# One Trainium2 core: attention's kv product moved beside the second half of a feed-forward block, queries transposed in pairs

## The chip, the cores and the metric

The kernel runs on one core of one Trainium2 chip. The metric is the device time of one execution in microseconds. Before the change it is 605.95 us, the median of three runs (605.42 to 606.97). A core has TensorE (PE; matmuls and, in a list of its own, their weight loads, PEld), VectorE (DVE), ScalarE (ACT), GpSimd (POOL) and SyncE (SP), which here issues every DMA.

## What is computed

```python
def _A_ref(x, wqkv, wo):                  # linear attention, H = 32 heads of Dh = 16
    qkv = (x @ wqkv).reshape(B, S, 3, H, Dh).transpose(2, 0, 3, 1, 4)
    q, k, v = qkv[0], qkv[1], qkv[2]
    phi = lambda t: jnp.where(t > 0, t + 1, jnp.exp(t)) + 1e-6
    pq, pk = phi(q), phi(k)
    kv = jnp.einsum("bhsd,bhse->bhde", pk, v)
    z = jnp.einsum("bhsd->bhd", pk)
    num = jnp.einsum("bhqd,bhde->bhqe", pq, kv)
    den = jnp.einsum("bhqd,bhd->bhq", pq, z)[..., None] + 1e-6
    return (num / den).transpose(0, 2, 1, 3).reshape(B, S, D) @ wo

xn = _layernorm(x)
s = _A_ref(xn, wqkv, wo)
g = _silu((_gelu(xn @ w_gate) * (xn @ w_up)) @ w_down)
out = x + s * g
```

The shapes are B = 1, S = 2048 tokens, D = 512, F = 1792, all in fp32.

## The kernel before, in words

**Products.** A large product is cut into 2 x 2 blocks and made with seven block products instead of eight (the table PRODUCTS; products 1 to 7 below are its entries), so sums and differences of blocks ("forms") are needed on both sides. Every fp32 form is split into a high and a low part of a type that TensorE multiplies in one pass, and a product is the sum of high x high, high x low and low x high: `sum3` (L508 is its matmul) issues three matmuls of 128x512 for each pair of operands. Splits are a cast on ScalarE (L486) and a subtraction on VectorE or GpSimd (L492).

**Stages.** (1) The start: 16 token tiles are normalised, transposed and turned into forms; k and q are projected, phi(q) goes to DRAM (`q_d`), and G = xnᵀ·phi(k) is summed in four PSUM banks and stored (`g_d`). v itself is never made: kv is the product of v's weights and G. (2) The feed-forward block in two halves of the tokens, p = 1 and then p = 0. Each has 14 "quads" (seven units of F, gate and up for each) of seven products, named FX, FY and FZ by their PSUM tiles, and the products with w_down in groups (DX, DY, DZ), added into `acc`. In half p = 1 the forms of the weights are made by GpSimd, ScalarE and VectorE from raw weights and stored to DRAM; half p = 0 loads them again (w, wd). At the boundary of the halves the forms of xn for the second half are loaded (Xh, Xl), and so far also GT and wv (`attn_loads`); `attn_first` sums z, makes kv (pkv, L1250; masked to each head's 16 x 16 block), multiplies it with wo to a matrix M (pm, L1264), and M's forms are made and stored (m_d). (3) `queries(i)`, eight times in half p = 0: two token tiles of phi(q) are loaded, multiplied with z on GpSimd (u), summed to den, inverted and normalised on VectorE, transposed on TensorE (ptq, L1165), copied by ScalarE and stored (pn_d). (4) The last stage: forms of pn times M's forms (ms) in four quads of two halves and two column blocks, SX, SY, SZ and SV by their tiles; `block` adds a product to a saved one, multiplies with silu of the feed-forward block (g, acc), adds x (xp) and stores.

**What sets the order.** Nothing is issued when it is written. `do` records each operation with its engine, a cost and what it reads and writes; class Plan then simulates all five engines, gives each operation a due time and lists it by these. The pe_keys rank TensorE's operations only as a first setting. STEPS is a list of random seeds: each one shifts the due times in a short stretch of the program by a random amount. So the order on every engine comes from the costs and STEPS together, and each engine, SP with its single DMA queue among them, executes its list strictly in turn. `in_turn` binds operations of given keys to a stated order.

**Places in SBUF and PSUM.** `D2(12)` to `D2(14)` are the three places RAW through which raw weights pass in half p = 1; queries use them for q, u and the transposed pT; before the change so do wv, wo, M and the temporaries of M's forms. `ring` hands out places in rotation, and an operation that reuses one waits for the last user. WAYS and ON_POOL say for each block of the last stage which engine multiplies ("C": GpSimd) and adds x, and "B" that the product is written over g.

The touched functions, with line numbers as in the profile:

## Time and profile before

| | before |
|---|---|
| median of three runs | 605.95 us |
| profiled execution: time | 606.77 us |
| profiled execution: span of the records | 605.10 us |
| TensorE busy | 593.9 us, 98% |
| weight loads | 489.1 us, 81% |
| VectorE busy | 479.0 us, 79% |
| GpSimd busy | 353.9 us, 58% |
| ScalarE busy | 336.2 us, 56% |
| granted TensorE clock, mean | 0.998 |
| moved by DMA | 143.14 MB, mean 237 GB/s |

The span runs from the first to the last record; 1.67 us of the profiled execution's time lie around it. In a row of the timeline stand the start, the busy time, the engine, line, operation, output<-inputs and the count; in brackets the engine's idle time ahead of it and what ended that. A matmul's record runs past its issue, so the next one's start shows the pitch better than the duration. In the rows of waits stand the total, the number and the longest. A DMA row gives the size of one transfer and the median time from issue to landing.

### The profile page before, as it was taken

Reading aid. Unit: us, or ns where it says so; the run is one execution under the profiler, and the core shown is the slowest. Engines: PE = TensorE matmul, PEld = TensorE weight load, DVE = VectorE, ACT = ScalarE, POOL = GpSimd, SP = SyncE. Lnnn points to the kernel's source line nnn. Section 1 sums busy time; section 2 is a strip of 40 time slices with the busy share of each in tenths; the row PEclk is TensorE's granted clock in tenths of the full one; section 3 lists DMA queues with packets and bytes.
Section 4 is the critical chain, followed back from the end, with each engine's and each line's share of the span. In section 5 each row is a group of like instructions: output and inputs, shape, how many; then the busy total and the mean of one; then the engine's idle time right before and its main releaser. Section 6 shows DMA issues by size and latency. Waiting matters only on the chain.

```text
span 605.1 us, 8228 instructions
## 1 busy us (share of the span) xinstructions
PE 593.9 (98%) x2696; PEld 489.1 (81%) x2696; DVE 479.0 (79%) x700; ACT 336.2 (56%) x610; POOL 353.9 (58%) x298
## 2 busy tenths in 40 slices
PE   8999999999999999999999999999999999999996
PEld 7888888888888888887888878788888888887875
DVE  6999988785688987889879654767865986587997
ACT  6767878866666744654554154645404550477740
POOL 3925754552588976876787042648704670559455
PEclk9999999999999999999999999999999999999999
DMA  7269621358648747863869879988639774998536
GB/s 257 83 210 305 207 71 71 121 165 324 225 157 310 264 157 265 326 223 125 285 242 354 310 249 414 407 278 271 197 134 323 244 238 130 323 309 308 199 131 251
DMA packets 58794, 143.14 MB, mean 237 GB/s; under 512 B 5504, under 2 KB 17024, under 8 KB 58752
## 3 DMA queue, kind: packets, MB, share of 16 engines
q1 hardware_dynamic: 58752, 142.63, 67.3%
q8 instruction: 21, 0.34, 0.2%
q14 instruction: 21, 0.17, 0.1%
HBM read 81.00 MB, written 61.60 MB: 236 GB/s over the span
## 4 chain that ended last, share of the span: by engine, by line
PE 85%; DMA 9%; DVE 3%; ACT 1%; issue 0%; SPq 0%; POOL 0%; DVEq 0%; ACTq 0%
PE FX L508 22%; PE DX L508 11%; PE FZ L508 11%; PE gps L508 7%; PE FY L508 6%; PE X L508 5%; PE DZ L508 5%; PE Z L508 3%; PE SX L508 3%; PE DY L508 2%; PE q L508 2%; DMA m_d<-m 2%; DMA GT<-g_d 1%; PE SZ L508 1%; PE k L508 1%; PE Y L508 1%
## 5 line engine op out<-in xcount | busy, mean ns | idle before, releaser
L508 PE MATMUL FX<-Xh,w 128*128 128x512 f32 x448 | 150.9, 390 | 0.0
L1073 POOL TENSOR_TENSOR h<-h,g 128x512 f32<-128x512 f32 x42 | 62.9, 1498 | 89.8 <-DVE h L492 81.0
L508 PEld LDWEIGHTS FX<-Xh,w 128*128 128x128 f32 x448 | 83.9, 188 | 17.6 <-DVE w L492 0.3
L492 POOL TENSOR_TENSOR h<-h,h 128x512 f32<-128x512 f32 x56 | 86.5, 1545 | 12.3 <-ACT g L1065 1.8
L508 PE MATMUL FX<-Xl,w 128*128 128x512 f32 x224 | 87.3, 390 | 0.0
L508 PE MATMUL FZ<-Xh,w 128*128 128x512 f32 x224 | 77.4, 391 | 0.0
L486 ACT COPY fu<-FX 128x512 f32<-128x512 f32 x56 | 32.9, 588 | 74.3 <-PE FX L508 60.3
L508 PE MATMUL gps<-pks,xns 128*128 128x512 f32 x192 | 51.0, 391 | 0.0
L508 PEld LDWEIGHTS FX<-Xl,w 128*128 128x128 f32 x224 | 42.1, 188 | 8.7
L508 PEld LDWEIGHTS FZ<-Xh,w 128*128 128x128 f32 x224 | 41.8, 188 | 8.5
L508 PE MATMUL FZ<-Xl,w 128*128 128x512 f32 x112 | 43.9, 392 | 0.0
L753 POOL TENSOR_TENSOR zacc<-zacc,kp 128x512 f32<-128x512 f32 x16 | 25.2, 1574 | 31.7 <-DVE kp L742 31.3
L1099 DVE TENSOR_TENSOR acc<-acc,DX 128x512 f32<-128x512 f32 x48 | 32.5, 683 | 13.2 <-PE DX L508 12.7
L508 PEld LDWEIGHTS gps<-pks,xns 128*128 128x128 f32 x192 | 35.8, 188 | 7.4
L508 PE MATMUL FY<-Xh,w 128*128 128x512 f32 x112 | 39.6, 394 | 0.0
L492 DVE TENSOR_TENSOR h<-fu,FZ 128x512 f32<-128x512 f32 x28 | 19.2, 685 | 18.5 <-PE FZ L508 9.4
L1065 ACT ACTIVATE g<-g 128x512 f32<-128x512 f32 x42 | 26.6, 633 | 12.4 <-DVE g L492 12.3
L1099 DVE TENSOR_TENSOR acc<-acc,DZ 128x512 f32<-128x512 f32 x32 | 21.8, 685 | 14.5 <-PE DZ L508 13.9
L508 PE MATMUL X<-kq,Xh 128*128 128x512 f32 x96 | 31.8, 397 | 0.0
L492 POOL TENSOR_TENSOR u<-q,zacc 128x512 f32<-128x512 f32 x16 | 22.0, 1395 | 13.6 <-DMA q<-q_d 13.4
L492 DVE TENSOR_TENSOR g<-fu,FZ 128x512 f32<-128x512 f32 x28 | 19.1, 683 | 13.0 <-PE FZ L508 7.1
L492 POOL TENSOR_TENSOR T<-xt 128x256 f32<-128x256 f32 x16 | 13.7, 856 | 19.6 <-DVE kq L492 11.5
(422 smaller groups left out, 1600.7 us busy)
## 6 DMA issues: line engine op xcount, KB each, us to landing
w_d<-w SPq DMA_DIRECT2D x36, 512.0 KB, 4.9
w<-w_d SPq DMA_DIRECT2D x36, 512.0 KB, 5.0
wd_d<-wd SPq DMA_DIRECT2D x21, 512.0 KB, 4.8
wd<-wd_d SPq DMA_DIRECT2D x21, 512.0 KB, 5.2
x<-in_first SPq DMA_DIRECT2D x16, 256.0 KB, 3.3
q_d<-qp SPq DMA_DIRECT2D x16, 256.0 KB, 2.3
q<-q_d SPq DMA_DIRECT2D x16, 256.0 KB, 4.3
pn_d<-pT SPq DMA_DIRECT2D x8, 512.0 KB, 5.5
```

The source lines that it names most:

```text
L486: do("ACT", act(n), lambda o, i: nc.scalar.copy(o, i), dst, src, name=name)
L492: do(eng, c, lambda o, p, q: getattr(e, f"tensor_{op}")(o, p, q), dst, a, b, name=name)
L508: nc.tensor.matmul(o, v[i], v[i + 1], start=start and part == 0 and i == 0, stop=stop and part == 1 and i == len(v) - 2, skip_group_check=on)
L753: do("POOL", pool(D), lambda o, i: nc.gpsimd.tensor_add(o, o, i), zacc, p0, name="zacc")
L1065: curved("gelu", do("ACT", curve(NC), lambda o, i: nc.scalar.activation(o, i, AF.Gelu_apprx_tanh), g, ps if e is None else g, name="gelu"))
L1073: do("POOL", pool(NC), lambda o, i: nc.gpsimd.tensor_mul(o, o, i), h, g, name="h")
L1099: do("DVE", dve(NC), lambda o, i: nc.vector.tensor_add(o, o, i), a, ps, name="acc")
```

## The change

(1) `attn_loads` and `attn_first` are cut up. `z_part` stays at the boundary. `kv_part`, recorded beside quad 5 of half p = 0, loads v's weights and G in four pairs through RAW (wvg0 to wvg3), and one TensorE operation for each pair adds its four products into one bank; `m_part` makes the mask, the masked kv and M, with two pairs of wo through RAW, and stores M's raw values to a new DRAM array (mr_d). `m_forms`, beside quads 6 and 8, loads them again, makes the forms and stores them. (2) In `queries` the transposes of both token tiles are one TensorE operation. The planner's cost for the transposes of xn at the start is also another. (3) In the last quad the bank Z is copied by ScalarE (sz5) ahead of its block (1,1), and the end is fixed as products 6, 5, 7, then 3, then the two halves of 4. (4) Three blocks of the last stage are done in other ways: (0,0,1) goes over g with its addition on GpSimd, (1,0,0) has its multiply on GpSimd, (1,1,1) returns to VectorE, and (2,1,1) adds on GpSimd. (5) STEPS is another list, so the order changes everywhere.

```diff
-    STEPS = (11, 15, 18, 27, 48, 58, 91, 94, 107, ...)
+    STEPS = (28, 30, 51, 59, 73, 79, 109, 133, 151, ...)
...
-        do("PE", 0.432, run, pt, xns[t], ident, key=("T", n, i), name="T")
+        do("PE", 0.52, run, pt, xns[t], ident, key=("T", n, i), name="T")
...
-            pt = bank(ring("ptq", [5, 6, 7]), f"ptq{t}", (P, KT, P))
...
-            do("PE", 0.432, run_t, pt, half(q, n), ident, key=("QT", i, n))
-            copy("ACT", pTs[:, :, n * P:(n + 1) * P], pt, D, "pqT")
+        pts = [bank(ring("ptq", [5, 6, 7]), f"ptq{t0 + n}", (P, KT, P)) for n in range(2)]
+
+        def run_t(o, a, b, c, idn):
+            for v, u in ((o, b), (c, a)):
+                for k in range(KT):
+                    nc.tensor.transpose(v[:, k, :], u[:, k * P:(k + 1) * P], idn)
+        do("PE", 0.95, lambda o, a, b, idn: run_t(o, b, a, pts[1](), idn), pts[0], half(q, 0), half(q, 1), ident, more=(pts[1],), key=("QT", i))
+        for n in range(2):
+            copy("ACT", pTs[:, :, n * P:(n + 1) * P], pts[n], D, "pqT")
...
+            if not p and n in BESIDE:
+                keys += BESIDE[n]()
...
+    def kv_part():
+
+        pkv = kv_state["pkv"] = bank(5, "pkv", (P, KT, P))
+        for c in range(KT):
+            t = raw_pair(f"wvg{c}")
+            dma(half(t, 0), ext(first[PLACE["v", c]]), 256)
+            dma(half(t, 1), g_d(c, (slice(None), c)), 256)
+
+            def run_kv(o, a, b, c=c):
+                for g in range(KT):
+                    nc.tensor.matmul(o[:, g, :], a[:, g * P:(g + 1) * P], b[:, g * P:(g + 1) * P],
+                                     start=(c == 0 and g == 0), stop=(c == KT - 1 and g == KT - 1), skip_group_check=True)
+            do("PE", 0.95, run_kv, pkv, half(t, 0), half(t, 1), key=("kv", c))
+        return [("kv", c) for c in range(KT)] + m_part()
+
+    def m_part():
+
         mask2 = U("fe", FE, "mask2", F32, (P, P))
         do("POOL", 1.5, make_mask, mask2)
...
+           kv4, kv_state["pkv"], mask2)
+        for a in range(2):
+            wo_t = raw_pair(f"wo{a}")
+            pms = []
+            for h in range(2):
+                g = 2 * a + h
+                dma(half(wo_t, h), ext(wo_k[:, g]), 256)
+                pms.append(bank(6 + h, f"pm{g}"))
+                do("PE", 0.95, lambda o, a, b, g=g: nc.tensor.matmul(o, a[:, g, :], b, start=True, stop=True),
+                   pms[-1], kv4, half(wo_t, h), key=("m", g))
+            raw = raw_pair(f"m{a}")
+            for h in range(2):
+                copy("ACT", half(raw, h), pms[h], D, "M")
+            dma(mr_d(a, a), raw, 512, "store")
+        return [("m", g) for g in range(KT)]
+
+    def m_forms(a):
+        raw = raw_pair(f"mr{a}")
+        dma(raw, mr_d(a, a), 512)
+        ws = weights("D", a + 1, f"m{a}")
+        make_weights(ws, raw, D_BLOCKS, f"m{a}")
+        keep_weights(("m", a), ws)
+        return []
+
+    mr_d = dram_view([2, P, 2, D], "mr_d", 2)
+    BESIDE = {5: kv_part, 6: lambda: m_forms(0), 8: lambda: m_forms(1)}
...
-    attn_loads()
-    raws = attn_first()
+    z_part()
...
-    for a in range(2):
-        ws = weights("D", a + 1, f"m{a}")
-        make_weights(ws, raws[a], D_BLOCKS, f"m{a}", 12)
-        keep_weights(("m", a), ws)
...
-    WAYS = {(1, 0, 0): "B", (1, 1, 1): "B", (2, 0, 1): "B", (2, 1, 0): "B", (2, 1, 1): "B", (3, 0, 0): "C", (3, 1, 1): "B"}
-    ON_POOL = ((1, 0, 0), (1, 1, 1), (2, 0, 1), (2, 1, 0), (3, 0, 0), (3, 1, 1))
+    WAYS = {(2, 1, 1): "B", (3, 0, 0): "C", (3, 1, 1): "B", (2, 0, 1): "B", (1, 0, 0): "C", (2, 1, 0): "B", (0, 0, 1): "B"}
+    ON_POOL = ((0, 0, 1), (1, 0, 0), (2, 0, 1), (2, 1, 0), (2, 1, 1), (3, 0, 0), (3, 1, 1))
...
+        z5 = esaved(Z, f"sz5_{n}") if last else Z
         prod_s(X, 7, False)
         u3 = esaved(X, f"su3_{n}")
-        block(1, 1, u3, Z, V)
+        block(1, 1, u3, z5, V)
...
-            pe_keys += [("S", p, c, i) for i in (6, 7, 5, 3)] + [("S", p, c, 4, h) for h in range(2)]
+            end = [("S", p, c, 3), ("S", p, c, 4, 0), ("S", p, c, 4, 1)]
+            pe_keys += [("S", p, c, i) for i in (6, 5, 7)] + end
+            in_turn(end)
```

The first place is SP's queue at the boundary. Before, G's pieces (GT, from g_d) and v's weights (wv) stand among the loads of X, and the first queries' load q8 stands far behind, among the stores of M's forms (m_d) and loads of weights:

```order
L461 DMA GT0_3327<-g_d_81 128x512
L461 DMA Xl0_265<-xl_d_83 128x1024
L461 DMA Xh0_251<-xh_d_82 128x1024
L461 DMA GT2_3340<-g_d_81 128x512
L461 DMA GT1_3347<-g_d_81 128x512
...
L461 DMA wv23_3368<-in_first 128x512 x2
L461 DMA GT3_3381<-g_d_81 128x512
...
L461 DMA wd61_3705<-wd61_d_160 128x512
L461 DMA m12_d_169<-m12_3673 128x1024
L461 DMA q8_3714<-q_d_80 128x512 x2
```

Now SP's queue has there:

```order
L461 DMA wd53_d_159<-wd53_3092 128x1024
L461 DMA draw6_3145<-in_w_down 128x1024
L461 DMA Xl0_268<-xl_d_83 128x1024
L461 DMA Xh0_255<-xh_d_82 128x1024
L461 DMA q8_3245<-q_d_80 128x512 x2
L461 DMA Xh0_255<-xh_d_82 128x1024
L461 DMA Xl0_268<-xl_d_83 128x1024
```

GT, wv, wo and M's stores are gone from the boundary, and q8's load stands behind the first two loads of X.

The second place is SP's queue near quads 7 and 6 of the second half (w7, w6), now: wvg2 takes the place that pT12, the transposed queries 12 and 13, leaves with the store to pn1_d.

```order
L461 DMA pn1_d_85<-pT12_4038 512x1x256
L461 DMA w70_4062<-w70_d_128 128x1024
L461 DMA w61_4074<-w61_d_125 128x512
L461 DMA wvg2_4087<-in_first 128x512
L461 DMA wvg2_4087<-g_d_81 128x512
L461 DMA w63_4104<-w63_d_127 128x1024
L461 DMA wvg3_4114<-in_first 128x512
L461 DMA wvg3_4114<-g_d_81 128x512
L461 DMA wo0_4123<-in_wo 128x512 x2
L461 DMA w72_4142<-w72_d_130 128x1024
L461 DMA w73_4162<-w73_d_131 128x1024
L461 DMA wo1_4168<-in_wo 128x512 x2
```

TensorE's list there, behind kv's last products, now:

```order
L1265 MATMUL pm0_4196<-wo0_4123,kv_4171 128x512
L508 MATMUL DX050_4186<-hf5l_3876,wd50_3376 128x512
L508 MATMUL DX050_4186<-hf5h_3850,wd50_3376 128x512
L508 MATMUL DX050_4186<-hf4h_4117,wd40_3812 128x512
L508 MATMUL DX050_4186<-hf4l_4126,wd40_3812 128x512
L508 MATMUL DX050_4186<-hf4h_4117,wd40_3812 128x512
L1265 MATMUL pm2_4211<-wo1_4168,kv_4171 128x512
L1265 MATMUL pm3_4215<-wo1_4168,kv_4171 128x512
```

M's four products stand between the feed-forward products, five of which separate pm0 from pm2 in the same bank.

The third place is the end of TensorE's list. Before, product 4's last half and then product 3 (SZ3):

```order
L508 MATMUL SX3_5663<-sf1l_5564,ms11_5257 128x256
L508 MATMUL SX3_5663<-sf1h_5540,ms11_5257 128x256
L508 MATMUL SZ3_5747<-sf0h_5488,ms03_5184 128x512
L508 MATMUL SZ3_5747<-sf1h_5540,ms13_5282 128x512
L508 MATMUL SZ3_5747<-sf0l_5530,ms03_5184 128x512
```

Now product 3 stands first:

```order
L508 MATMUL SZ3_5733<-sf0h_5476,ms03_5186 128x512
L508 MATMUL SZ3_5733<-sf1l_5563,ms13_5290 128x512
L508 MATMUL SZ3_5733<-sf1h_5547,ms13_5290 128x512
L508 MATMUL SX3_5689<-sf0h_5476,ms01_5216 128x256
L508 MATMUL SX3_5689<-sf1h_5547,ms11_5267 128x256
L508 MATMUL SX3_5689<-sf0l_5533,ms01_5216 128x256
```

The last twelve matmuls are now the 256-wide ones of product 4.

More of the change, by code (lines that the diff above doesn't have):

```diff
@@ L90 @@
     MARGIN = (0.1, 0.12, 1.0)
-    STEPS = (11, 15, 18, 27, 48, 58, 91, 94, 107, 139, 141, 151, 155, 162, 166, 191, 202, 212, 236, 256, 276, 286, 297, 319, 368, 377, 416, 480, 534, 563, 568, 579, 592, 611, 642, 646, 658, 672, 802, 821, 826, 849, 874, 909, 952, 1020, 1026, 1073, 1136, 1137, 1185, 1259, 1319, 1349, 1358, 1387, 1603, 1666, 1738, 1786, 1808, 1933, 1950, 2048, 2049, 2106, 2116, 2119, 2242, 2344, 2373, 2500, 2681, 2855, 2879, 3018, 3170, 3177, 3271, 3305, 3351, 3481, 3531, 3656, 3716, 3717, 3810, 4131, 4199, 4404, 4448, 4462, 4630, 4657, 4723, 4913, 5502, 5645, 5850, 6356, 6465, 6550)
+    STEPS = (28, 30, 51, 59, 73, 79, 109, 133, 151, 156, 172, 196, 242, 268, 273, 283, 305, 321, 344, 349, 369, 373, 379, 396, 407, 410, 416, 442, 471, 488, 517, 546, 586, 603, 690, 731, 752, 755, 789, 806, 811, 885, 999, 1028, 1071, 1082, 1197, 1229, 1260, 1313, 1328, 1454, 1461, 1487, 1505, 1523, 1531, 1582, 1598, 1619, 1714, 1744, 1809, 1825, 1884, 1908, 2199, 2256, 2425, 2509, 2559, 2587, 2830, 2905, 3004, 3279, 3386, 3411, 3415, 3433, 3457, 3592, 3702, 3921, 4000, 4006, 4030, 4174, 4182, 4277, 4425, 4583, 4716, 5136, 5149, 5175, 5225, 5401)
     WAIT = 0.3
@@ L1157, in queries @@
         for n in range(2):
-            t = t0 + n
             do("DVE", 0.602, lambda o, j: nc.vector.scalar_tensor_tensor(
                 o, o, EPS, j.unsqueeze(2).to_broadcast([P, H, DH]), op0=ALU.add, op1=ALU.mult), heads(half(q, n)), r[:, n], name="pn")
-            pt = bank(ring("ptq", [5, 6, 7]), f"ptq{t}", (P, KT, P))
-            def run_t(o, a, b):
+        pts = [bank(ring("ptq", [5, 6, 7]), f"ptq{t0 + n}", (P, KT, P)) for n in range(2)]
+        def run_t(o, a, b, c, idn):
+            for v, u in ((o, b), (c, a)):
                 for k in range(KT):
-                    nc.tensor.transpose(o[:, k, :], a[:, k * P:(k + 1) * P], b)
-            do("PE", 0.432, run_t, pt, half(q, n), ident, key=("QT", i, n))
-            copy("ACT", pTs[:, :, n * P:(n + 1) * P], pt, D, "pqT")
+                    nc.tensor.transpose(v[:, k, :], u[:, k * P:(k + 1) * P], idn)
+        do("PE", 0.95, lambda o, a, b, idn: run_t(o, b, a, pts[1](), idn), pts[0], half(q, 0), half(q, 1), ident, more=(pts[1],), key=("QT", i))
+        for n in range(2):
+            copy("ACT", pTs[:, :, n * P:(n + 1) * P], pts[n], D, "pqT")
         j = t0 % 8
@@ L1190, in ffn @@
                     queries(i)
-                    keys += [("QT", i, m) for m in range(2)]
+                    keys.append(("QT", i))
             if not is_up and len(todo) > 1 and todo[0][-1] != u and ("F", p, 2 * todo[0][-1] + 1, 3) in keys:
@@ L1203, with raw_pair @@
     wo_k = wo.rearrange("(k p) n -> p k n", p=P)
-    def attn_loads():
-        gt = [U("fg", FG, f"GT{c}") for c in range(KT)]
-        wv = [D2(12, "wv01"), D2(13, "wv23")]
-        wo_t = D2(14, "wo01")
-        for c in range(KT):
-            dma(gt[c], g_d(c, (slice(None), c)), 256)
-        for c in range(KT):
-            dma(half(wv[c // 2], c % 2), ext(first[PLACE["v", c]]), 256)
-        for c in range(2):
-            dma(half(wo_t, c), ext(wo_k[:, c]), 256)
-        kv_state["gt"] = gt
-        kv_state["wv"] = [half(wv[c // 2], c % 2) for c in range(KT)]
-        kv_state["wo"] = [half(wo_t, c) for c in range(2)]
+    def raw_pair(name):
+        return D2(ring("raw", RAW), name)
     def make_mask(o):
@@ L1225, in make_mask, with z_part @@
                                 pattern=[[DH, P // DH], [0, DH]], channel_multiplier=-1)
-    def attn_first():
+    def z_part():
         ones_r = U("fe", FE, "ones_r", F32R, (P, P))
@@ L1242, in attn_first @@
+    def m_part():
         mask2 = U("fe", FE, "mask2", F32, (P, P))
         do("POOL", 1.5, make_mask, mask2)
-        pkv = bank(1, "pkv", (P, KT, P))
         kv = U("fe", FE, "kv")
         kv4 = kv.map(lambda ap: ap.rearrange("p (g d) -> p g d", g=KT))
-        for g in range(KT):
-            def run_kv(o, *v, g=g):
-                for c in range(KT):
-                    nc.tensor.matmul(o[:, g, :], v[c][:, g * P:(g + 1) * P], v[KT + c][:, g * P:(g + 1) * P],
-                                     start=(c == 0), stop=(c == KT - 1))
-            do("PE", 0.9, run_kv, pkv, *kv_state["wv"], *kv_state["gt"], key=("kv", g))
@@ L1253, in attn_first @@
-        do("DVE", dve(D), lambda o, i, m: nc.vector.tensor_mul(o, i, m.unsqueeze(1).to_broadcast([P, KT, P])),
-           kv4, pkv, mask2)
-        raws = []
-        wo23 = D2(12, "wo23")
-        for c in range(2):
-            dma(half(wo23, c), ext(wo_k[:, 2 + c]), 256)
-            kv_state["wo"].append(half(wo23, c))
-        for g in range(KT):
-            if not g % 2:
-                raws.append(D2(13 + g // 2, f"m{g}"))
-            pm = bank([4, 1, 4, 1][g], f"pm{g}")
-            do("PE", 0.86, lambda o, a, b, g=g: nc.tensor.matmul(o, a[:, g, :], b, start=True, stop=True),
-               pm, kv4, kv_state["wo"][g], key=("m", g))
-            copy("ACT", half(raws[g // 2], g % 2), pm, D, "M")
@@ L1267, in attn_first @@
-        return raws
+        do("DVE", dve(D), lambda o, i, m: nc.vector.tensor_mul(o, i, m.unsqueeze(1).to_broadcast([P, KT, P])),
+           kv4, kv_state["pkv"], mask2)
[12 more added lines that the diff above has]
+            dma(mr_d(a, a), raw, 512, "store")
@@ L1277 @@
     dk = down_keys(1, todo[0])
-    pe_keys += dk[:6] + ["z"] + [("kv", g) for g in range(KT)] + dk[6:] + [("m", g) for g in range(KT)]
+    pe_keys += dk[:6] + ["z"] + dk[6:]
     for n, key in enumerate(KEYS):
         dma(g1_d(n, n), acc[1, key], 256, "store")
-    for a in range(2):
-        ws = weights("D", a + 1, f"m{a}")
-        make_weights(ws, raws[a], D_BLOCKS, f"m{a}", 12)
-        keep_weights(("m", a), ws)
     for s in (0, 1, 4, 3, 5, 6, 2):
```

## The prediction

> **What bounds the kernel now.** I read the page's engine row first, then TensorE's own waits, then the table by stage.

> ```profile
> PE 593.9 (98%) x2696; PEld 489.1 (81%) x2696; DVE 479.0 (79%) x700; ACT 336.2 (56%) x610; POOL 353.9 (58%) x298
> ```

> TensorE is busy 98% of the span. The change keeps every matmul and transpose, so it can win only idle time of TensorE and what follows its last matmul. The view of TensorE's waits names all of the idle time that matters here:

> ```profile
> PE ptq L1165 <- DVE q L1159: 1.1, 1, 1.1
> ...
> PE pkv L1250 <- DMA GT<-g_d: 1.0, 1, 1.0
> PE DX L508 <- ACT hf0h L486: 0.5, 1, 0.5
> PE SZ L508 <- DVE SV L492: 0.4, 1, 0.4
> PE k L508 <- DVE Xl L492: 0.3, 1, 0.3
> ...
> PE k L508 <- ACT b L486: 0.2, 1, 0.2
> ```

> The ptq, pkv and SZ waits stand at places that the change rewrites. The table by stage (core time, then TensorE, weight loads, VectorE, ScalarE, GpSimd, each with its count, granted clock, DMA share, GB/s) says what is scarce there:

> ```profile
> 355.00:385.00 30.00, 28.89 (x130) 23.70 (x129) 16.74 (x24) 14.90 (x27) 16.69 (x16) 1.00 1.02 388
> 385.00:440.00 55.00, 55.00 (x254) 45.53 (x253) 42.64 (x60) 28.61 (x51) 32.89 (x23) 1.00 0.78 265
> ...
> 563.00:590.00 27.00, 26.74 (x118) 21.50 (x116) 26.31 (x43) 14.30 (x27) 12.72 (x9) 1.00 0.45 156
> ```

> Around the boundary of the halves the DMA engines are full (1.02); in the stretch to which the work moves they are at 0.78 and TensorE never idles; in the last stage VectorE is full, 26.31 of 27.00 us. The clock is full everywhere, so I work in time alone. For the pitch of a 512-wide matmul I take a dense piece of the chain:

> ```profile
> 356.54 2.72 PE FX L508 x12
> ```

> 2.72 / 12 = 0.2267 us.

> **(a) kv's wait goes: -1.13.** TensorE's rows at the boundary:

> ```profile
> 336.19 0.83 PE L1250 MATMUL pkv<-GT,wv 128*128 128x128 f32 x6
> 337.99 3.14 PE L1250 MATMUL pkv<-GT,wv 128*128 128x128 f32 x26 [0.97 <-DMA GT<-g_d]
> 340.89 0.48 PE L508 MATMUL DX<-hf6l,wd 128*128 128x512 f32 x1
> ```

> The island lasts 340.89 - 336.19 = 4.70. Its dense part makes 26 records in 340.89 - 337.99 = 2.90, 0.1115 each; all 32 need 3.57. So 4.70 - 3.57 = 1.13 is wait: the last GT chunk stands in the queue behind X loads that wait for their places. In the new order nothing reads GT or wv before the fourth quad of the second half, so this wait goes whole; what the kv work may wait for at its new place is (f).

> **(b) The first queries' wait goes: -1.26.**

> ```profile
> 360.99 9.13 DMA m_d<-m
> ...
> 370.18 8.15 DMA q<-q_d
> ```
> ```profile
> 382.67 0.39 PE L508 MATMUL FZ<-Xh,w 128*128 128x512 f32 x1
> 384.16 0.66 PE L1165 MATMUL ptq<-ident,q 128*128 128x128 f32 x4 [1.11 <-DVE q L1159]
> ...
> 386.04 0.60 PE L1165 MATMUL ptq<-ident,q 128*128 128x128 f32 x4
> 386.39 0.48 PE L508 MATMUL DX<-hf6h,wd 128*128 128x512 f32 x1
> ```

> From the last FZ to the transposes pass 384.16 - 382.67 = 1.49; 0.23 of it is that matmul, 1.26 is wait. The chain shows where it comes from: q's place is freed by the store of M's forms (9.13), then q's load takes 8.15 in full DMA, then come the queries' own VectorE steps. In the new order M's stores are gone from here, and q8's load stands right behind the first two X loads, some 30 us ahead of its transposes. Were it to take 8.15 again, it would be hidden; I take the whole 1.26.

> **Pairing by itself: nothing.** A group of four transposes costs 386.39 - 386.04 = 0.35 and makes the next matmul 0.09 slower (0.32 to the following one against 0.23): 0.44. The trace also holds two groups that stand together:

> ```profile
> 534.19 1.04 PE L1165 MATMUL ptq<-ident,q 128*128 128x128 f32 x8
> 534.98 0.70 PE L508 MATMUL FZ<-Xh,w 128*128 128x512 f32 x2
> ```

> Eight cost 0.79 plus the same 0.09, 0.88 = 2 x 0.44. The planner's other transpose costs change only places.

> **(c) The last stage's stall: -0.54, at worst nothing.**

> ```profile
> 589.35 0.39 PE L508 MATMUL SX<-sf1h,ms 128*128 128x512 f32 x1
> 590.12 0.50 PE L508 MATMUL SZ<-sf0h,ms 128*128 128x512 f32 x1 [0.38 <-DVE SV L492]
> ```
> ```profile
> 589.38 0.69 DVE L492 TENSOR_TENSOR SV<-su,SZ 128x512 f32<-128x512 f32 x1
> 589.98 0.69 DVE L492 TENSOR_TENSOR sf0l<-pb,sf0h 128x512 fp32r<-128x512 f32 x1
> ```

> The gap is 0.77, less a pitch of 0.23: 0.54. TensorE may not write the bank SZ before VectorE has read it into SV. In the new order product 3 of this quad comes six matmuls later (6 x 0.2267 = 1.36) and VectorE's SV stands one operation later (0.60, from the two rows' starts), so there is 0.76 more room than 0.54 asks. VectorE loses two operations in this stage net (1.2 us of a full engine), GpSimd gains two. Zero is the other bound: a full VectorE may arrive as late as before.

> **(d) Start-up: -0.2 (-0.5 to +0.5).** ScalarE's casts are put in another order.

> ```profile
> 12.41 0.62 ACT L486 CAST kq<-wq 128x512 fp32r<-128x512 f32 x1 [1.34 <-DMA wq<-in_first]
> ...
> 13.72 0.37 ACT L486 CAST b<-pt 128x256 fp32r<-128x256 f32 x1
> ```

> The cast of b ends TensorE's last start-up wait (0.2), and it stands behind a cast that waited 1.34 for wq2; wq2 is now loaded ahead of wq1's second half. I take the 0.2. Downwards the waits on b and Xl (0.2 and 0.3) bound it; upwards the copy of xt, now ahead of the first cast of Xh (0.5 of ScalarE), which a filler-padded start may absorb or not.

> **(e) The tail: +0.45 (+0.1 to +0.7).** TensorE's last matmul and VectorE's end before:

> ```profile
> 599.37 0.39 PE L508 MATMUL SZ<-sf1h,ms 128*128 128x512 f32 x1
> ```
> ```profile
> 598.40 0.89 DVE L492 TENSOR_TENSOR SX<-acc,SX 128x256 f32<-128x256 f32 x2
> 599.39 0.75 DVE L492 TENSOR_TENSOR xp<-xp,SX 128x256 f32<-128x256 f32 x2
> ...
> 600.78 0.70 DVE L492 TENSOR_TENSOR SZ<-acc,SZ 128x512 f32<-128x512 f32 x1
> 601.51 0.69 DVE L492 TENSOR_TENSOR xp<-xp,SZ 128x512 f32<-128x512 f32 x1
> ```

> With E the end of the last matmul (599.76), VectorE ended at 602.20 = E + 2.44. Now product 3 comes first and the two 256-wide halves last, which seems to leave less behind E; but VectorE still has the whole of quad (1,1)'s and (0,1)'s blocks ahead of the halves. Product 7 ends six wide and twelve half-wide matmuls before E (1.36 + 1.44 = 2.8), its bank is copied (0.59 and a hand-over), so SV3's add can begin at about E - 1.9; then follow at 0.60 each the multiply, SZ3's add and multiply to E + 0.6, a half's multiply (0.445), xp01's add (0.60), the other half's multiply (0.445) and two adds of 0.375: E + 2.85. Against 2.44 that is +0.4 to +0.45; the store behind it is half as large and I give it no credit. The bounds: each dependent step at 0.73 (601.51 - 600.78) instead of 0.60 gives +0.7; an SV3 that starts 0.3 earlier gives +0.1.

> **(f) Waits of the new chain: +0.3 (0 to 1.6).** kv's third pair of operands goes into the place of the transposed queries 12 and 13. It waits for two ScalarE copies of these, their store, and its own load; medians from the DMA views, first of the new stretch, then of the boundary:

> ```profile
> q<-q_d SPq DMA_DIRECT2D x4, 256.0 KB, 4.0
> pn_d<-pT SPq DMA_DIRECT2D x2, 512.0 KB, 5.1
> ```
> ```profile
> m_d<-m SPq DMA_DIRECT2D x6, 512.0 KB, 8.3
> ...
> GT<-g_d SPq DMA_DIRECT2D x4, 256.0 KB, 7.8
> ```
> ```profile
> L486 ACT COPY fu<-FX 128x512 f32<-128x512 f32 x56 | 32.9, 588 | 74.3 <-PE FX L508 60.3
> ```

> Copies 2 x 0.59 and a hand-over 1.3, store 5.1, issue 0.4 (estimated), load 4.0: 10.8. TensorE meanwhile has 42 products and 16 kv records: 42 x 0.2267 + 16 x 0.1115 = 11.3. Slack 0.5. The second pair of wo goes into kv's last place: 0.4 + 4.0 = 4.4 against 16 products and two of M's (3.63 + 1.72) = 5.4. Slack 1.0. While SP stands at the third pair's load, w63, the fourth pair and both wo loads queue behind it. M's products share two banks, so pm2 waits for ScalarE's copy of pm0 (0.59 and a hand-over) against five products (1.13). Each alone holds; with three slacks of 0.4 to 1.0 in one chain I expect 0.3 to be lost. Upwards, one load taking the boundary's 7.8 with the store at 5.1 would be 3.3 on kv; half of such an excess, 1.6, is my bound. M's round trip through memory (two stores, two loads of 512 KB) and its forms have over ten microseconds until the last stage loads them.

> The wait on hf0h (0.5) I leave as it is: its producers keep their order. **Sum**: -1.13 - 1.26 - 0.54 - 0.2 + 0.45 + 0.3 = -2.38. The profiled execution's span 605.10 becomes 602.7, its time 606.77 becomes 604.4. It lies 0.82 above the median of the runs, so against 605.95 the forecast is **603.6**, with its own range 602.0 to 605.0.

> **The rivals.** *Slower: the new chain waits.* If loads at the new place take what they took at the boundary, kv's third pair is ready after 1.3 + 8.3 + 0.4 + 7.8 = 17.8, a wait of 6.5, and wo's second pair costs 0.4 + 7.8 - 5.4 = 2.8: -2.38 - 0.3 + 9.3 = +6.6, **612.5**. It decides from 4.5 us of waits on, where the other terms (-2.68) are used up and 0.3% passed. For it: all is behind one queue, and weight loads of the same quads share it. Against it: 0.78 of DMA and 4.0 us per load in the very stretch. Chance 0.11.

> *No change: a wait takes the place of the removed ones.* Start-up +0.5, stall unchanged, tail +0.7 and chain +1.0 to 1.6 give -1.13 - 1.26 + 0.5 + 0.7 + 1.0 = -0.2, **605.8**. The same comes out if the first queries still wait (1.26) and the rest goes half well. For it: the whole order is a new one, and each slack was planned, not measured. Chance 0.20.

> *GpSimd takes back what VectorE is given.* VectorE's operations on two SBUF tiles stretch while GpSimd runs:

> ```profile
> 581.70 1.63 DVE L492 TENSOR_TENSOR sf1l<-pb,sf1h 128x512 fp32r<-128x512 f32 x1
> ```
> ```profile
> 579.90 2.88 POOL L492 TENSOR_TENSOR pb<-pb 128x512 f32<-128x512 f32 x2
> ```

> 1.63 against the usual 0.69 (as SV's). Two more GpSimd operations then cost VectorE up to 2 x 0.94 = 1.9, more than the 1.2 saved; the SZ stall stays (+0.54) and the tail is the longer one (+0.25): -1.6, **604.3**. Against it: the added GpSimd work can fall beside operations that read PSUM. Chance 0.12. [...]

> **How the numbers follow.** Forecast 0.57, GpSimd 0.12, no change 0.20, slower 0.11. A measurement of this kernel can tell about 0.3% from no change, that is 604.1 and 607.8. Faster: 0.53 of the forecast, 0.05 of GpSimd, together 0.58. Slower: 0.11, with 0.01 from the no-change case, 0.12. The rest, 0.30, is the same. The range runs from 602.0 (stall and waits gone, tail +0.1, start-up -0.5, no loss in the chain: -3.3, and some more) to 606.4, beyond the no-change case; 612.5 is left out.

> **What would show it.** In the profile after: pkv's records in four groups of eight between products without a wait over 0.3; no ptq wait on q; GT and wv gone from the boundary, q's first load well under 8 us away from its use; SZ's stall gone; VectorE ending about E + 2.85; idle time of TensorE some 2.9 less in the middle. A wait of TensorE on wvg or wo above 2 us, a new X or w wait behind the blocked SP queue in the fourth to sixth quad, or a start-up longer by 1 us would make it wrong.

## The result and the profile after

The change makes the kernel slower: 613.66 us against 605.68 us (medians of four runs each), a ratio of 1.0135 with a 95% interval of 1.0111 to 1.0158. The forecast was 603.6, faster. The profiled execution after took 613.60 us; its span is 611.9 us, 6.8 more than before.

The page's engine row and TensorE's waits after:

```profile
PE 595.7 (97%) x2696; PEld 491.0 (80%) x2696; DVE 482.1 (79%) x698; ACT 337.8 (55%) x611; POOL 361.6 (59%) x300
```
```profile
PE FX L508 <- ACT fu L486: 2.4, 1, 2.4
PE ptq L1165 <- DVE q L1158: 1.5, 1, 1.5
...
PE pkv L1245 <- DMA wvg<-g_d: 0.8, 1, 0.8
PE k L508 <- DVE Xl L492: 0.6, 1, 0.6
```

The waits on GT, on the first queries, on SZ, hf0h and acc are all gone. Three new ones stand in the second half. In TensorE's timeline they are:

```profile
413.64 0.40 PE L508 MATMUL FZ<-Xh,w 128*128 128x512 f32 x1
414.79 1.13 PE L1245 MATMUL pkv<-wvg 128*128 128x128 f32 x8 [0.76 <-DMA wvg<-g_d]
...
464.43 0.39 PE L508 MATMUL FZ<-Xh,w 128*128 128x512 f32 x1
466.31 1.09 PE L1165 MATMUL ptq<-ident,q 128*128 128x128 f32 x8 [1.49 <-DVE q L1158]
...
538.47 0.39 PE L508 MATMUL DX<-hf1h,wd 128*128 128x512 f32 x1
541.24 0.74 PE L508 MATMUL FX<-Xh,w 128*128 128x512 f32 x2 [2.38 <-ACT fu L486]
...
542.06 0.60 PE L508 MATMUL FX<-Xh,w 128*128 128x512 f32 x1
...
545.44 0.43 PE L508 MATMUL FZ<-Xl,w 128*128 128x512 f32 x1
...
602.33 0.28 PE L508 MATMUL SX<-sf1h,ms 128*128 128x256 f32 x1
```

Less a pitch of 0.23 each, they cost 0.92, 1.65 and 2.54 us. From 542.06 to 545.44 there are eight matmuls in 3.38 us instead of 1.81: another 1.6. TensorE's granted clock was at half there, 0.50 from 542.07 to 545.48 (the last section has the row). Together 6.7, and start-up is 0.3 longer. Against that stand the removed 1.13, 1.26 and 0.54, and, by the same measure, 0.69 (hf0h) and 0.39 (acc): 4.0. So TensorE should end 3.0 later; it ends at 602.61 instead of 599.76, 2.85 later.

The other 4.0 us lie behind TensorE's end. VectorE's and SyncE's last rows after:

```profile
604.86 0.75 DVE L492 TENSOR_TENSOR xp<-xp,SX 128x256 f32<-128x256 f32 x2
```
```profile
571.55 0.33 SPq L461 DMA_DIRECT2D xp<-in_xt  x1
588.12 0.81 SPq L461 DMA_DIRECT2D out_y<-xp  x2
590.79 1.64 SPq L461 DMA_DIRECT2D xp<-in_xt  x2
592.53 0.37 SPq L461 DMA_DIRECT2D out_y<-xp  x1
599.51 0.33 SPq L461 DMA_DIRECT2D xp<-in_xt  x1
599.93 7.63 SPq L461 DMA_DIRECT2D out_y<-xp  x10
```

VectorE ends at 605.61, 3.0 behind TensorE instead of 2.44. The span ends 6.3 after VectorE; before it was 2.9. SyncE's rows of before say why:

```profile
568.52 0.33 SPq L461 DMA_DIRECT2D xp<-in_xt  x1
577.81 0.34 SPq L461 DMA_DIRECT2D out_y<-xp  x1
582.41 0.33 SPq L461 DMA_DIRECT2D xp<-in_xt  x1
...
593.70 0.38 SPq L461 DMA_DIRECT2D xp<-in_xt  x1
596.31 6.25 SPq L461 DMA_DIRECT2D out_y<-xp  x9
```

The first store left at 577.81 and now leaves at 588.12; the last load of x left at 593.70 and now at 599.51; the ten last stores queue behind that load. SyncE's waits after name what held the first store, the addition of x that edit (4) gave to GpSimd; what this addition costs by itself is measured below:

```profile
SPq L461 <- POOL xp L492: 17.4, 3, 16.2
```

### The profile page after: what moved, and what is told of

Its sections match the earlier page's. It is cut to its first block, busy times and chain, and to the rows that moved or that the text cites. A ratio compares the mean times of both kernels' runs of the same rounds, so it can differ in the third digit from the quotient of the medians.

```text
span 611.9 us, 8235 instructions
## 1 busy us (share of the span) xinstructions
PE 595.7 (97%) x2696; PEld 491.0 (80%) x2696; DVE 482.1 (79%) x698; ACT 337.8 (55%) x611; POOL 361.6 (59%) x300
## 5 line engine op out<-in xcount | busy, mean ns | idle before, releaser
L508 PE MATMUL FX<-Xh,w 128*128 128x512 f32 x448 | 151.7, 391 | 2.4 <-ACT fu L486 2.4
L508 PEld LDWEIGHTS FX<-Xh,w 128*128 128x128 f32 x448 | 83.8, 188 | 20.3 <-ACT fu L486 3.2
L1073 POOL TENSOR_TENSOR h<-h,g 128x512 f32<-128x512 f32 x42 | 61.5, 1468 | 64.3 <-DVE h L492 62.8
L492 POOL TENSOR_TENSOR h<-h,h 128x512 f32<-128x512 f32 x56 | 85.9, 1534 | 15.3 <-DVE hf2l L492 5.0
L508 PE MATMUL FX<-Xl,w 128*128 128x512 f32 x224 | 87.7, 392 | 0.0
L508 PE MATMUL FZ<-Xh,w 128*128 128x512 f32 x224 | 78.8, 393 | 0.0
L486 ACT COPY fu<-FX 128x512 f32<-128x512 f32 x56 | 32.9, 587 | 65.8 <-PE FX L508 57.0
L508 PE MATMUL gps<-pks,xns 128*128 128x512 f32 x192 | 52.4, 393 | 0.1
L508 PEld LDWEIGHTS FZ<-Xh,w 128*128 128x128 f32 x224 | 42.4, 190 | 9.2 <-DVE g L492 0.4
L508 PEld LDWEIGHTS FX<-Xl,w 128*128 128x128 f32 x224 | 42.2, 188 | 9.0 <-issue 0.2
L492 POOL TENSOR_TENSOR u<-q,zacc 128x512 f32<-128x512 f32 x16 | 22.5, 1427 | 42.7 <-DMA q<-q_d 21.4
L508 PE MATMUL FZ<-Xl,w 128*128 128x512 f32 x112 | 44.1, 393 | 0.0
L508 PEld LDWEIGHTS gps<-pks,xns 128*128 128x128 f32 x192 | 35.8, 188 | 7.5 <-PE fill L530 0.2
L753 POOL TENSOR_TENSOR zacc<-zacc,kp 128x512 f32<-128x512 f32 x16 | 23.8, 1489 | 28.8 <-DVE kp L742 24.4
L508 PE MATMUL FY<-Xh,w 128*128 128x512 f32 x112 | 39.2, 391 | 0.0
L492 DVE TENSOR_TENSOR h<-fu,FZ 128x512 f32<-128x512 f32 x28 | 19.1, 684 | 22.6 <-ACT fu L486 13.1
L508 PE MATMUL X<-kq,Xh 128*128 128x512 f32 x96 | 31.8, 395 | 0.0
L492 DVE TENSOR_TENSOR g<-fu,FZ 128x512 f32<-128x512 f32 x28 | 19.1, 682 | 13.3 <-PE FZ L508 7.2
L486 ACT COPY fe<-FX 128x512 f32<-128x512 f32 x28 | 16.4, 587 | 18.2 <-PE FX L508 17.7
## 6 DMA issues: line engine op xcount, KB each, us to landing
w_d<-w SPq DMA_DIRECT2D x36, 512.0 KB, 5.2
w<-w_d SPq DMA_DIRECT2D x36, 512.0 KB, 5.3
wd_d<-wd SPq DMA_DIRECT2D x21, 512.0 KB, 4.9
wd<-wd_d SPq DMA_DIRECT2D x21, 512.0 KB, 4.9
x<-in_first SPq DMA_DIRECT2D x16, 256.0 KB, 3.3
q_d<-qp SPq DMA_DIRECT2D x16, 256.0 KB, 2.3
q<-q_d SPq DMA_DIRECT2D x16, 256.0 KB, 4.4
pn_d<-pT SPq DMA_DIRECT2D x8, 512.0 KB, 5.6
```

Source lines behind the costliest of these rows:

```text
L486: do("ACT", act(n), lambda o, i: nc.scalar.copy(o, i), dst, src, name=name)
L492: do(eng, c, lambda o, p, q: getattr(e, f"tensor_{op}")(o, p, q), dst, a, b, name=name)
L508: nc.tensor.matmul(o, v[i], v[i + 1], start=start and part == 0 and i == 0, stop=stop and part == 1 and i == len(v) - 2, skip_group_check=on)
L753: do("POOL", pool(D), lambda o, i: nc.gpsimd.tensor_add(o, o, i), zacc, p0, name="zacc")
L1073: do("POOL", pool(NC), lambda o, i: nc.gpsimd.tensor_mul(o, o, i), h, g, name="h")
```

## Experiments

### One stall after the other, with the order otherwise kept

Theory A: the loss lies in single places of the order, where an instruction waits at the head of an in-order engine. Four kernels move a few operations of the changed kernel in its finished order. The edits are shortened here, two of them into words.

The first moves the addition for block (0,0,1) back to VectorE:

```diff
                 tt("POOL" if (n, dh, th) in ON_POOL else "DVE", "add", x, x, cut(r, h, m), w, "xr")
+                # block (0,0,1): planned as before, issued on VectorE right behind its multiply
+                nc.vector.tensor_add(x, x, r)
```

> The changed kernel with one operation moved: the addition of x for block (0,0,1) of the last stage's first quad runs on VectorE right behind its multiply, not on GpSimd behind two forms; every other operation keeps its place. Theory A (SyncE stands 16.2 us at the first store for that GpSimd addition, and x's loads and the last stores queue behind it): the first store leaves at about 583.5 instead of 588.1, x's last load some 4 to 5 us earlier, and the time falls by 2.5 to 3.5 us, to 610.2 to 611.2. Rival B (the last stores are slow because VectorE ends late and is full): VectorE gets 0.6 us more to do, the time changes by less than 0.6 us.

Measured: 613.24 us (611.62 to 615.34), 0.4 less, which is within the spread. The store did leave earlier (584.62), and the span ended 6.9 behind TensorE instead of 9.3. But VectorE had no room for the operation. TensorE was as far as in the changed kernel up to 586 us and lost 1.9 from there to its end, half of it at once:

```profile
588.03 0.50 PE L508 MATMUL SX<-sf1l,ms 128*128 128x512 f32 x1 [0.95 <-DVE sf1l L492]
```

So theory A's mechanism is there, and rival B's full engine too; the 2.4 us won behind TensorE were lost ahead of its end.

The second:

```diff
+    cast = first operation named "s0h"          # Xh<-pb100 on ScalarE
+    behind([cast], third ScalarE operation after it)   # with what depends on it
```

> The changed kernel with ScalarE's cast of the first form of pb100 put behind the three copies that stood behind it (fu and two of pT). Theory A (TensorE's 2.54 us wait at 538.5 is this cast's wait for pb's load, and the slow matmuls after it are its consequence): both go, 3.0 to 3.8 us less, 609.9 to 610.7. Rival B (what is late there is all that needs loads; the next reader stands in its place): less than 1 us gained.

Measured: 612.14, 1.5 less, between the two forecasts, with a wide spread (610.84 to 616.11). The profiled execution is the fastest of the four. In it the 2.38 on fu is gone and so are the slow matmuls, but 1.03 us have come back on another engine, since VectorE's subtraction of the same form still stood ahead of the feed-forward block's h:

```profile
542.23 0.74 PE L508 MATMUL FZ<-Xh,w 128*128 128x512 f32 x2 [1.03 <-DVE h L492]
```

The third:

```diff
+    turn = the operation with key ("QT", 4)
+    behind([turn], fourth TensorE operation after it)  # twelve matmuls
```

> The changed kernel with the transposes of the fifth pair of queries put twelve matmuls (2.7 us) later on TensorE. Theory A (they stood 1.65 us for a q load that takes longer than planned): the wait goes, 1.4 to 1.7 us less, 612.0 to 612.3. Rival B (q's place is single, so the next pair is late by as much and waits in turn): no gain, 613.3 to 614.

Measured: 615.38 (613.83 to 617.54); no gain. The wait on q is gone from TensorE, and a longer one (2.2, on ScalarE's fu) stands one group of matmuls further on. GpSimd's and VectorE's queues of the changed kernel show what stands behind q's load there:

```profile
460.47 2.54 POOL L492 TENSOR_TENSOR u<-q,zacc 128x512 f32<-128x512 f32 x2 [5.24 <-DMA q<-q_d]
462.97 1.28 POOL L1073 TENSOR_TENSOR h<-h,g 128x512 f32<-128x512 f32 x1
```

GpSimd has stood 5.24 us for the load, and the feed-forward block's own product h waits behind it; on VectorE h stands behind den and the normalised q, and ScalarE's copy fu behind h's cast. Moving the one instruction of TensorE frees none of these.

The fourth makes all three moves:

> The three moves together in the changed kernel; nothing of the change is undone but the engine of one addition. Theory A (the loss lies in the order at these places, not in the moved work): the gains add, -7.2 to -8.8 us, 604.9 to 606.5, about the kernel before. Rival B (the moved work itself costs, by 2 MB more of transfers and more GpSimd work, and waits reappear elsewhere): 609 or more.

Measured: 615.47 (614.60 to 618.50). The profiled execution is the slowest of the five, and 3.4 us of it are half clock (546.19 to 553.02), 1.7 more than in the changed kernel; without that the gains are missing too. Theory A is wrong in its simple form: a late transfer blocks several in-order engines at once (q's load held GpSimd for 5.24 us, and VectorE and ScalarE stood behind), and the gains of the single moves didn't add. These kernels also repeat the changed kernel's first 460 us unaltered, so they measure the new kv chain four times more. TensorE's waits on wvg there:

```profile
412.02 1.13 PE L1245 MATMUL pkv<-wvg 128*128 128x128 f32 x8 [0.26 <-DMA wvg<-g_d]
```
```profile
416.27 1.13 PE L1245 MATMUL pkv<-wvg 128*128 128x128 f32 x8 [2.18 <-DMA wvg<-g_d]
```

The first row is of the first kernel and waits for kv's third pair, the second is of the third kernel and waits for the fourth. In the five profiles of this piece TensorE waits 0 to 0.5 us for the third pair and 0 to 2.2 for the fourth, in one and the same order: the chain has no slack, so each transfer's scatter is seen.

### Each part alone, in orders without seeds

Every part changes the whole order, and the two lists STEPS were searched for two different kernels. With an empty list both are planned alike. The eight kernels are the kernel before with every choice of three parts of the diff: kv and M moved (K), transposes in pairs with the planner's new cost (P), the last stage's edits 3 and 4 (L).

```diff
-    STEPS = (...)
+    STEPS = ()
```

> The kernel before with an empty list STEPS, so with the planner's order and no seeds; the base for the next three, which have an empty list too. Both theories: somewhat slower than the kernel before, 607 to 613, since the seeds were picked for it.

> The kernel before with only kv and M moved into the second half, empty STEPS. Theory A (the moved work makes the three places RAW, which kv's operands, wo, M and its forms now share with the queries' q, u and transposed q, a chain without slack, with every load 4 to 5 us in one SyncE queue): 3 to 6 us above the base, with waits of TensorE on wvg and q between 400 and 470. Rival B (the move itself is fine, the new list of seeds gave an order that does not fit the chip): 1 to 2.5 us below the base, the two waits at the boundary gone and less than 1 us of new ones.

> The kernel before with only the transposes in pairs (and the planner's other cost for a transpose), empty STEPS. Theory A (the first tile's transposes now wait for the second, which lengthens each pair's hold on the RAW places by about 1 us): 0 to 2 us above the base, a wait on q at one or two pairs. Rival B: within 0.7 us of the base.

> The changed kernel with an empty list STEPS. Theory A (the cost lies in what was changed): 5 to 9 us above the base, as the changed kernel stands to the kernel before. Rival B (it lies in the seeds): within 2 us of the base.

> The kernel before with only the last stage's edits (WAYS, ON_POOL, sz5, the fixed end), empty STEPS; the base has 611.3, with its stores done 5.3 us after TensorE's last matmul. Theory C (GpSimd's addition of x for block (0,0,1) holds the first store, and with it x's loads and the last stores): the first store leaves 3 us or more later against TensorE's end than in the base, 2 to 3.5 us above the base, 613 to 615. Rival (the edits free VectorE as intended): 0.5 to 2 us below the base.

> kv moved and transposes in pairs, the old last stage, empty STEPS. Theory D (alone each costs nothing, 609.9 and 610.8, but together a pair's longer hold on the RAW places and kv's pieces there wait for each other): 612 to 616, with waits on wvg or q above 1 us. Rival (no interaction, the whole loss is in the last stage): 608.5 to 611.

> Transposes in pairs and the last stage's edits, kv where it was, empty STEPS. Theory C: 612.5 to 615, like the last stage's edits alone. Theory D: the same. Rival of both (only the order's luck decides): anywhere from 608 to 617, and not the sum of the two alone.

> kv moved and the last stage's edits, transposes one by one, empty STEPS. Theory C: 1.4 below the kernel with the last stage's edits alone, 611 to 613.5. Theory D: the same, since the pairing is missing. Rival: as for the run before, not the sum.

| parts | median us | | parts | median us |
|---|---|---|---|---|
| none | 611.27 | | L | 613.63 |
| K | 609.85 | | K, L | 612.45 |
| P | 610.76 | | P, L | 611.50 |
| K, P | 615.73 | | K, P, L | 617.71 |

Read in pairs: without P the move of kv gains 1.4 and 1.2 us; with P it costs 5.0 and 6.2. P alone gains 0.5 and, with L, 2.1; beside K it costs 5.9 and 5.3. L costs 2.4, 2.6 and 2.0, beside P alone 0.7. The runs of one kernel spread by 1.0 to 4.7 us, so the small steps are not clear of noise. Theory A's 3 to 6 us for K alone did not come. The loss of the whole change stands without any seeds (+6.4, as against +8.0 with the two lists). Theory C's cost of the last stage is there: with L the first store leaves 14.8 to 16.5 us ahead of TensorE's end instead of 20.0 to 20.2, and the span ends 6.8 to 8.3 us behind it instead of 5.3 to 5.6. For P and L together, though, both theories had 612.5 or more; 611.50 came about because TensorE ended earlier there. The interaction of K and P is the largest effect, 6.4 us of the medians and, with L, 7.4.

In the profiled executions more than half of it is clock, not waiting. There the interaction is 615.6 - 607.5 - 609.5 + 610.0 = 8.6 us of the spans. TensorE's granted clock falls to half for stretches of 3.41 us, each of which costs up to 1.7, half its length: two in K, P, one in the kernel without any part (341.04 to 344.45), none with K alone or P alone. That is up to 5.1 of the 8.6. With L it is the same: twice the length in K, P, L, one stretch in L, none in the other two. The runs lean the same way: the mean clock of K's is 0.998 to 0.999, of K, P's 0.992 to 1.0, and the run at 1.0 is its fastest, 613.14. The two of K, P, in a table by stretch (the clock is the third number from the end):

```profile
154.92:158.34 3.42, 3.42 (x10) 2.67 (x9) 2.52 (x4) 1.49 (x3) 0.92 (x1) 0.50 0.65 261
421.16:424.58 3.42, 3.42 (x13) 3.03 (x14) 0.00 (x0) 0.00 (x0) 0.00 (x0) 0.50 0.55 199
```

Theory D's own mechanism, waits for places, shows only in part. Waits of TensorE without any part, with P alone, and with K and P:

```profile
PE ptq L1165 <- DVE q L1159: 1.9, 1, 1.9
```
```profile
PE FZ L508 <- DVE g L492: 2.0, 1, 2.0
```
```profile
PE pkv L1245 <- DMA wvg<-g_d: 2.7, 2, 1.6
PE FZ L508 <- DVE g L492: 2.2, 2, 2.0
...
PE ptq L1165 <- DVE q L1158: 1.5, 3, 0.6
```

In both, P's order has a stall of 2.0 us on g in the first half; with P alone the clock stays full behind it, with K and P the first of the two stretches follows. With P alone the wait on q that the kernel without any part has at the boundary is missing, so the stall is nearly free, perhaps because TensorE arrives later there; with K no wait at the boundary is left that could go, and the waits on wvg and q come on top. How much of the rest is the queries' longer hold on the three places RAW and how much another order, these runs don't separate.

### The last stage's addition by itself

> The kernel before with one operation moved, the reverse of the first experiment: the addition of x for block (0,0,1) runs on GpSimd behind the last form of pb001 (the multiply writes over g), everything else in its place. Theory C (this addition holds SyncE's first store, behind which x's loads and the last stores queue): the first store leaves at about 584.2 instead of 577.8 and the time rises by 1.5 to 3.5 us, to 607.2 to 609.2. Rival (the stores have room, and VectorE gains 0.6 us): 605.0 to 606.3.

This is the kernel before with its own seeds and one operation moved; the multiply ahead of it writes over g because GpSimd reads it from there.

```diff
+                # block (0,0,1), in the finished order:
+                nc.vector.tensor_mul(g, g, Z)        # was: Z = g * Z
+                nc.gpsimd.tensor_add(x, x, g)        # was on VectorE; now behind the last form of pb001
```

Measured: 610.59 against 605.41, a ratio of 1.0094 (1.0061 to 1.0127): +5.2 us for one addition, more than theory C's 1.5 to 3.5. The clock is full up to TensorE's end in both profiles, and GpSimd is busy for 353.9 us in both. SyncE's waits in this kernel, then its rows and TensorE's last:

```profile
SPq L461 <- POOL xp L1374: 12.7, 1, 12.7
```
```profile
583.09 0.34 SPq L461 DMA_DIRECT2D out_y<-xp  x1
...
597.36 0.34 SPq L461 DMA_DIRECT2D xp<-in_xt  x1
597.80 7.30 SPq L461 DMA_DIRECT2D out_y<-xp  x9
```
```profile
597.89 0.39 PE L508 MATMUL SZ<-sf1h,ms 128*128 128x512 f32 x1
```

TensorE ends at 598.28, no later than before, and the span of 608.4 ends 10.1 us after it instead of 5.3. Every load of x for the last half needs a place that a store must first leave; stores and loads share one queue; so a store that leaves 5.3 us later at its head pushes what is behind it: the last load left 6.1 us before TensorE's end and now leaves 0.9 before it. VectorE's 0.6 us of relief don't show.

### The order planned for later landings

The planner adds 1.0 us to each transfer's landing. In the moved chain's stretch loads take more than it reckons: by its constants a load of 256 KB lands after 0.72 + 256/400 + 0.8 + 1.0 = 3.2 us, and the loads of wvg and wo took 5.3 in the changed kernel. Four kernels have this margin at 3.0 and seeds searched for them; a fifth, the first below, has the usual margin and searched seeds.

```diff
-    MARGIN = (0.1, 0.12, 1.0)
+    MARGIN = (0.1, 0.12, 3.0)
```

> The kernel before with only kv and M moved, with a list STEPS searched for it as the lists of the two kernels are (seeds kept when they shorten the planned order). Theory D (the move alone is good for about 1.4 us where orders are of one kind): 603.5 to 605.3. Rival (the searched order is planned too tight for the loads of the moved work): 606.5 to 610, with waits on wvg and q above 1 us each.

Measured, kv and M moved, usual margin: 607.75, a ratio of 1.0031 (1.0013 to 1.0049). This is in the rival's range, though its waits on wvg and q, 0.8 and 0.6 us, are smaller than the rival had them.

> The same, but the planner reckons each transfer's landing 3.0 us late instead of 1.0, and seeds are kept when they shorten the order so reckoned. Theory E (transfers in the second half land 4 to 5 us after issue, the planner has about 2 to 3 with its margin, and each miss stands in an in-order engine): 1 to 4 us faster than with the usual margin, 602 to 605. Rival (landing times are not what the order misses): equal or slower than with the usual margin.

Measured, the same with landings 3.0 us late: 603.84, a ratio of 0.9966 (0.9952 to 0.9979). This is faster than both kernels. TensorE's waits behind the start-up, and the loads of its kv stretch:

```profile
PE SZ L508 <- DVE SV L492: 0.4, 1, 0.4
PE pm L1264 <- DMA wo<-in_wo: 0.4, 1, 0.4
```
```profile
wo<-in_wo SPq DMA_DIRECT2D x4, 256.0 KB, 6.7
...
wvg<-g_d SPq DMA_DIRECT2D x3, 256.0 KB, 5.2
pn_d<-pT SPq DMA_DIRECT2D x1, 512.0 KB, 6.6
```

The same rows of the changed kernel:

```profile
wvg<-g_d SPq DMA_DIRECT2D x4, 256.0 KB, 5.3
wo<-in_wo SPq DMA_DIRECT2D x4, 256.0 KB, 5.3
...
pn_d<-pT SPq DMA_DIRECT2D x1, 512.0 KB, 6.0
```

The loads are no quicker, yet nothing but 0.4 on wo waits for them: they are issued far enough ahead.

> The control for the fastest run so far (kv moved, 603.84): the kernel before, nothing of the change, with the planner's landing 3.0 us late and seeds searched for it in the same way. Theory F (the gain over the kernel before is the move of kv, the two boundary waits of 1.1 and 1.3 us): 605.0 to 606.5. Rival (the gain is the planner's later landing alone): 602.5 to 604.5.

Measured, nothing of the change: 605.70, a ratio of 1.0001 (0.9987 to 1.0015). So in the kernel before the later landing gives nothing, and the 1.9 us between these two fit kv's move, as theory F has it. Each of these kernels is one searched order, though: how much of the 3.9 us between 607.75 and 603.84 is the margin, and how much the luck of a search, stays open.

> The whole change, planned and searched with landings 3.0 us late. Theory E: the waits on wvg, q and pb shrink to under 0.5 us each, 607 to 610.5 against 613.7; what is left over the kernel before is the last stage. Rival (the places themselves are too few, so no order fits): 612 or more.

Measured, the whole change: 608.63, 5.0 less than the changed kernel. The waits on wvg and q are gone there, as theory E had it. A fresh search with the usual margin was not made for this kernel, so the 5.0 are margin and search together. In the profiled execution a wait of 1.8 on g is left, and a half-clock stretch behind it (153.97 to 157.38).

> The whole change with late landings and searched seeds, but block (0,0,1) of the last stage left on VectorE as in the kernel before. Theory C (the one addition on GpSimd holds the stores): 4 to 5 us less than with it (608.63), 603.5 to 605. Rival (the rest of the last stage's edits or the pairing cost the difference): 606.5 to 609.

Measured, without the addition of (0,0,1) on GpSimd: 607.43, only 1.2 less, in the rival's range. The first store does leave earlier, 22.0 us ahead of TensorE's end instead of 16.9, but the span ends 5.2 us behind TensorE instead of 5.8. So the late store costs 0.6 us here: with it the last load of x still left 6.7 us ahead of TensorE's end, where in the order of before it left 0.9 ahead. What a late store costs depends on the order behind it. What keeps this kernel 3.6 us above kv's move alone (pairs, the other edits of the last stage, the order) lies ahead of TensorE's end, since that kernel's span ends 5.3 behind it too, and is not separated.

## Why the prediction was wrong

- **(a) and (b), -1.13 and -1.26: right.** Both waits are gone in the trace after, and with the last stage as it was, between two orders searched in the same way, the move is worth 1.9 us (603.84 against 605.70), of 2.39 predicted less 0.3 for (f).
- **Pairing, nothing: right alone, wrong in company.** Alone it is -0.5. Beside the moved kv it is +5.9 and +5.3; of the 8.1 us between the profiled spans of K and K, P, up to 3.4 are half clock. The step costed the transposes themselves and not what else the pair and the planner's other cost move: a stall of 2.0 us on g comes with it, and behind that stall the clock was at 0.50 for 3.42 us in K, P and full with P alone.
- **(c), -0.54: right in place.** SZ's stall is gone. That VectorE is full was right too: 0.6 us put back on it cost TensorE 1.9.
- **(d), -0.2: missed by half a microsecond, inside its bounds** (+0.3).
- **(e), +0.45: right for VectorE, wrong for the end.** VectorE ended at E + 3.0 (E + 2.85 predicted). The step that failed is "the store behind it is half as large and I give it no credit": it took the stores as they were. They cost 3.4 us more. I had counted GpSimd's two added operations only as relief or contention for VectorE, and not asked which store waits for them, though SyncE's queue with the order store, load of x, store was there to read.
- **(f), +0.3 with 1.6 as the bound: mis-sized.** In five profiles of that same piece the waits on wvg are 0.3 to 2.2 in all. The third pair, whose slack the sum worked out, is waited for 0 to 0.5; most of the wait is for the fourth (up to 2.2), which the prediction named as queued behind it and gave no sum. The loads took 5.3 and the store 6.0 where the rows of before had 4.0 and 5.1 in this stretch; the prices were read where the moved traffic was not yet. Slacks of 0.4 to 1.0 against such a scatter are none.
- **What was left out: 1.65 + 2.54 + 1.6.** The other waits of the new order were taken to be like the old ones. They came where a q or pb load holds GpSimd, VectorE or ScalarE and the feed-forward block's work stands behind. The traffic between 435 and 470 us rises from 7.64 to 10.11 MB, and about 1.8 of it are the stores and the load of the moved M; with the plan made for later landings the waits on wvg and q are gone. The 1.6 is the clock: the step "the clock is full everywhere, so I work in time alone" held for the kernel before and not behind a new gap of 2.77 us.
- **The rivals.** The slower one gave 612.5 for kv's and wo's waits; 613.66 came about by other waits. It had the right cause, loads that take longer than planned behind one queue, and looked for it in one chain only. The GpSimd rival saw the contention: in the profile before, VectorE's 128x512 operations on two SBUF tiles took 0.67 to 0.69 us with GpSimd idle and as much as 1.78 beside it (at 300.86), those that read PSUM 0.67 to 0.70 either way; after, GpSimd's two additions of g to x took 1.83 each instead of 1.29 and 1.30. But it priced this on VectorE; the price was SyncE's queue.

## What to carry to other kernels

Of an operation moved to a slower or busier engine, ask first which DMA waits for its result, and what stands behind that DMA in its queue: one addition moved cost 5.2 us with no engine the busier for it. A part that is free alone can cost in company; but before such a difference is put down to the edit, the granted clock by stretch should be read, since here up to 5.1 of 8.6 us of it were half clock. Here transfers landed with such a scatter that the waits on wvg were 0.3 to 2.2 us in five profiles of one order; with slacks of 0.4 to 1.0 the order waited somewhere each time, and moving single waiting instructions didn't cure it; the orders searched for later landings did.

## What the runs showed that I had not expected

```profile
542.07:545.48 3.41, 3.41 (x10) 2.67 (x9) 1.25 (x2) 1.85 (x4) 3.41 (x3) 0.50 0.64 194
```
```profile
467.71:471.12 3.41, 3.41 (x11) 2.65 (x10) 1.88 (x2) 1.27 (x3) 3.25 (x3) 0.50 0.93 324
```
```profile
543.27 0.39 PE L508 MATMUL DX<-hf1h,wd 128*128 128x512 f32 x1
546.55 0.74 PE L508 MATMUL FX<-Xh,w 128*128 128x512 f32 x2 [2.89 <-ACT fu L486]
547.13 0.40 PE L508 MATMUL FX<-Xl,w 128*128 128x512 f32 x1
547.36 0.40 PE L508 MATMUL FX<-Xh,w 128*128 128x512 f32 x1
```

In the third experiment a gap of 3.28 us left the pitch at 0.23, while a gap of 2.60 us earlier in it, at 466.37, was followed by half clock from 469.96 to 473.37. Counted on in steps of 3.41 us from this fall, a border lies at 545.05 and cuts the longer gap into two parts of about 1.5 us; the three gaps that halved the clock lie whole in the 3.41 us ahead of the fall. So gaps of 2.49, 2.60 and 2.77 us cost up to 1.7 more each and one of 3.28 nothing more; that this goes by where a gap happens to fall is my estimate from these four. How much idle time in one such stretch is enough, these traces don't settle: in the first experiment about 2.1 us at 540.48 did nothing.
